# Decode attention over a sliding window: slabs of four (entry, head) pairs, a ring of three, a q projection that streams wq, and scores ordered by quadrant

## The chip, the cores and the metric

The kernel runs on one core of one Trainium2 chip. The metric is the device time of one execution in microseconds. A core has TensorE (PE in the profile; its weight loads are listed as PEld), VectorE (DVE), ScalarE (ACT), GpSimd (POOL) and SyncE (SP), which here issues nearly all DMAs. Each engine works through its own list of instructions in order and waits on semaphores. DMAs run on 16 DMA engines beside them. Data is worked on in SBUF (128 partitions); TensorE writes to PSUM, in banks of 512 fp32 per partition.

## What is computed

Two independent problems A and B of the same shape, whose results stand side by side in the output. Each is one decode step of attention with 32 query heads and 16 key/value heads for a batch of two, over the last 4096 positions of the cache.

```python
B, Sq, D = 2, 1, 576
Hq, Hkv, Sk, Dh = 32, 16, 16384, 128
W = min(4096, max(256, Sk // 4))              # 4096
q = (x @ wq).reshape(B, Sq, Hq, Dh)           # wq: 576 x 4096
k = jnp.repeat(k_cache[:, :, Sk - W:, :], 2, axis=1)
v = jnp.repeat(v_cache[:, :, Sk - W:, :], 2, axis=1)
scores = jnp.einsum("bhqd,bhkd->bhqk", q, k) * (Dh ** -0.5)
p = softmax(scores)
o = jnp.einsum("bhqk,bhkd->bhqd", p, v)
out = o.reshape(B, Sq, Hq * Dh) @ wo          # wo: 4096 x 576
```

All of it is bf16. Each key and value is used for two query heads only, so nearly all of the work is to bring in the windows of k and v: 2 problems x 2 tensors x 32 (entry, head) pairs of 1 MB.

## The kernel before

**Slabs.** A slab holds the windows of one kv head for both entries: two (entry, head) pairs, 2 MB, partition `2*r + b` holding 64 consecutive positions of entry b in one row of 16 KB. There are 32 K slabs and 32 V slabs. They go through one ring of five slots (`NR`). The order of transfers is K0, K1, ... with V(s-5) behind K(s) (`LS` = 5). SP issues them in that order (`issue_slab`, L273), and the transfer into a slot waits for the last reader of the slab that lay there: for K the last of its transposes, for V its second PV operation. The weights are threaded into the same queue: wq of A ahead of K0, wq of B in five parts (L282, L283) ahead of K7 to K11, and 1.2 MB of wo for each group of four slabs (L297). The last V slab comes in four pieces (L266).

**Scores.** K lies with positions on partitions, but the product with q needs the head dimension there. VectorE transposes blocks of 32x32 fp32 words, that is of pairs of bf16 (L844), 512 words per partition at a time, four per half slab (a unit, t). After that a partition holds a pair of dimensions of one block, and an element's position, parity and entry lie along the row. So a score matmul (L867) reads its moving operand with a step, and four of them (`p4`: two halves of the dimension, two parities) are needed for one entry of a unit. Their weights `zq` are q spread into 128 columns, nearly all zeros, so that each unit's scores land in their own rows of a PSUM bank `ST` that collects a group: eight units, four slabs.

```python
b0 = xt[:, c, o:o + 1]
mv = bass.AP(b0.tensor, b0.offset, [list(b0.ap[0]), [128, NJ], [4, 16]])
```

**Softmax** of a group: the row maximum (L378), a PE transpose (L382), a maximum over units and its negative (L392, L402), a PE broadcast (L407), its copy (L420), exp on ACT with the row sums (L428), a VectorE transpose (L476) and two products with a mask that lay the probabilities out as `pC` (L491), later the sums (L432 to L464). These steps are not done in one go: tables `pe_pre`, `da_pre`, `da_mid` and `da_post` place each of them at a unit and a quarter (t, q) of the loop (L694 to L736), so that scores and transposes of the next units stand between them on PE and VectorE.

**PV** (probability times V, L786): the weights are 16 columns of `pC`, the moving operand is 512 columns of V, and four matmuls write to four column blocks of `ACC`, side by side. It runs `LAG` = 11 units behind the transposes. ACT or VectorE copies the sum (L802, L804), four small matmuls (L758) combine the blocks into `OT`, VectorE normalises (L561).

**Projections.** q: for each group, 8 heads x 5 pieces of the dimension, wq as 128x128 weights and x as a moving operand of 56 columns, 40 matmuls (L513), then four selecting matmuls (L527) and ACT copies (L517, L545). The groups of A come at t = 0, 2, 4, 6, those of B at t = 24 to 27 and so on. Output: for each group but the last, the normalised rows are spread and redistributed (L625, L634, L646) and multiplied with wo in 16 matmuls (L658).

Of the kernel before, what the change touches and what calls it, by code (L numbers as in the profile page):

```python
# [59 lines left out]
def build_kernel(nc, probs, out, cfg=None):  # L60
    cfg = dict(cfg or {})
    NR = cfg.get("NR", 5)
    NKT = cfg.get("NKT", 3)
    NTB = cfg.get("NTB", 2)
    NZQ = 2
    ZW = 144
    LAG = cfg.get("LAG", 11)
    NPT = 3
    NS = cfg.get("NS", 56)
    LS = cfg.get("LS", 5)  # L70
    WQ_AT = cfg.get("WQ_AT", 7)
    QP_AT = cfg.get("QP_AT", 24)
    WO_LEAD = cfg.get("WO_LEAD", 5)
# [9 lines left out]
    NJ = W // 128  # L83
    assert NJ == 32
    NQ = 4
    NJ2 = 2 * NJ
    NRW = 64
    SLABW = NJ2 * 128
    UW = NJ * 128
    PP = Bb * Hkv  # L90
    NP = PP * NPROB
    ND = NP // 2
    NG = NP // 8
    GPP = PP // 8
    KP = PP // 2
    NK = NP // 2
    NFC = D // 128
    DREM = D - 128 * NFC
    assert DREM * 2 == 128
    HH = HD // 2  # L100
    NCH = NFC + 1
    NXC = NFC + 2
    NOUT = wo0.shape[1]
    NH = (NOUT + 1) // 2
    ACC0 = 128
    assert NOUT % 2 == 0 and ACC0 + NH <= 512 and NS <= 64 and NS % 2 == 0
    SCALE = float(Dh) ** -0.5
    PW = 512
    PIECES = [(0, 32), (32, 48), (48, 56), (56, 64)]

    def slab_info(D_):
        return D_ // Hkv, D_ % Hkv
# [5 lines left out]
    with es:  # L118
# [3 lines left out]
        xt = sb("xt", [128, NKT, UW], BF16)  # L122
# [3 lines left out]
        xT = sb("xT", [128, NPROB, NXC, 64], BF16)  # L126
        x_dup = sb("x_dup", [Bb, NPROB, 2, DREM, 2], BF16)
        x_sb = sb("x_sb", [Bb, NPROB, D], BF16)
        ident_b = sb("ident_b", [128, 192], BF16)
        zq = sb("zq", [128, 4, NZQ, 8, ZW], BF16)  # L130
        pR = sb("pR", [128, 2, PW], BF16)
        pT = sb("pT", [128, 2, 2 * PW], BF16)
# [3 lines left out]
        sel = sb("sel", [128, 4, 128], BF16)  # L136
        qT_sb = sb("qT_sb", [128, NG, 64], BF16)
# [8 lines left out]
        oTn = sb("oTn", [128, 2, 2, Bb], BF16)  # L146
# [3 lines left out]
        maskS = sb("maskS", [128, 8], BF16)  # L150
        selL = sb("selL", [128, 240], BF16)
        acc_sb = sb("acc_sb", [128, 2, 512], BF16)
        ident_r = sb("ident_r", [128, 72], BF16)
        pC = sb("pC", [128, NPT, 4, 2, NJ, 4], BF16)
        mask_bh = sb("mask_bh", [128, Bb, 2], BF16)
        out_sb = sb("out_sb", [Bb, NPROB, NOUT], BF16)
        ps = lambda name, shape: es.enter_context(nc.psum_tensor(name, shape, FP32))
        TB = [ps("tb%d" % i, [128, 512]) for i in range(NTB)]
        assert NTB == 2
# [9 lines left out]
        x_sems = [sem("xload%d" % P) for P in range(NPROB)]  # L169
        out_sem = sem("outdone")  # L170
        lastq_sem = [sem("lastq%d" % q_) for q_ in range(4)]
# [10 lines left out]
        p_ones_b = S.add("pool", lambda e: e.memset(ones_b[:], 1.0), [], "ones_b")  # L182
        def f_identb(e):
            e.affine_select(ident_b[:, 0:128], ones_b[:], [[-1, 128]], ALU.is_equal, 0.0, base=0, channel_multiplier=1)
            return e.memset(ident_b[:, 128:192], 0.0)
        p_ident_b = S.add("pool", f_identb, [p_ones_b], "ident_b")
        p_zqT = S.add("pool", lambda e: e.memset(qT_sb[:].rearrange("d g w -> d (g w)"), 0.0), [], "zero_qT")
        p_zxT = S.add("pool", lambda e: e.memset(xT[:].rearrange("c p h w -> c (p h w)"), 0.0), [], "zero_xT")

        def zq_zero(eng, zr_, p4s, tag):  # L190
            ops_ = []
            for p4 in p4s:
                ops_.append(S.add(eng, lambda e, p4=p4: e.memset(zq[:, p4, zr_, :, :].rearrange("d l w -> d (l w)").bitcast(FP32), 0.0),
                                  [], "%s_%d" % (tag, p4)))
            return ops_
        p_zq = {0: zq_zero("pool", 0, (2, 3), "zero_zq0p")}

        def f_sel(e):
            last = None
            for p4 in range(4):  # L200
                b32, par = p4 // 2, p4 % 2
                last = e.affine_select(sel[:, p4, :].rearrange("d (a p) -> d a p", a=4), ones_b[:, :].rearrange("d (a p) -> d a p", a=4),
                                       [[0, 4], [-2, 32]], ALU.is_equal, 0.0, base=-(64 * b32 + par), channel_multiplier=1)
            return last
        p_sel = S.add("pool", f_sel, [p_ones_b], "sel")
        p_ones_f = S.add("pool", lambda e: e.memset(ones_f[:], 1.0), [], "ones_f")
        p_ident_f = S.add("pool", lambda e: e.affine_select(ident_f[:], ones_f[:], [[-1, 128]], ALU.is_equal, 0.0,
                                                           base=0, channel_multiplier=1), [p_ones_f], "ident_f")
        for zr_ in range(1, NZQ):
            p_zq[zr_] = zq_zero("pool", zr_, (0, 1, 2, 3), "zero_zq%d" % zr_)  # L210

        p_zq[0] = p_zq[0] + zq_zero("dve", 0, (0, 1), "zero_zq0d")
        init_zero = {}
        init_zero["ST0"] = S.add("dve", lambda e: e.memset(ST[0][:], 0.0), [], "zero_ST0")
        late_zero = [("ST1", ST[1]), ("OT0", OT[0]), ("OT1", OT[1]), ("ACC0", ACC[0]), ("ACC1", ACC[1])]

        x_sem = x_sems[0]

# [7 lines left out]
        stream = []  # L226
        for s_ in range(ND + LS):
            if s_ < ND:
                stream.append(("K", s_))
            if s_ >= LS:  # L230
                stream.append(("V", s_ - LS))
        slab_idx = {key: n for n, key in enumerate(stream)}
        w_at = {}
        for P in range(NPROB):
            t0 = 0 if P == 0 else WQ_AT + 4 * GPP * (P - 1)
            for ch in range(NCH):
                w_at.setdefault(t0 + (0 if P == 0 else ch), []).append(("wq", P, ch))
        for G in range(NG):
            w_at.setdefault(4 * G + LS + (2 if by_group(G) else -1), []).append(("wo", G, 0))

        slab_dma = {}
        slab_quarters = {}
        slab_last_reader = {}
        wq_dma = {}
        wo_dma = {}
        qproj = {}
        qproj_ev = {}
        proj = {}
        next_stream = [0]

        def issue_slab(s):
            kind, D_ = stream[s]
            P, g = slab_info(D_)
            src_t = probs[P][1] if kind == "K" else probs[P][2]
            src = src_t[:, g, Sk - W:Sk, :].rearrange("b (r j) d -> r b (j d)", r=NRW)
            r = s % NR
            deps = []
            if s >= NR:
                assert slab_last_reader.get(s - NR) is not None, ("ring too small / order", s)
                deps = [slab_last_reader[s - NR]]  # L260

            if s == len(stream) - 1:
                qops = []
                for n_, (ja, jb) in enumerate(PIECES):
                    def fq(e, r=r, src=src, n_=n_, ja=ja, jb=jb):
# [64 lines left out]
        def tb_job(fn, tag, deps):  # L330
# [4 lines left out]
            if n >= NTB:  # L335
                d.append(tb_consumer[n - NTB])
# [657 lines left out]
```

## Time and profile before

| | |
|---|---|
| median of 3 runs | 373.14 us (372.84 to 373.9) |
| the profiled execution | 373.62 us |
| its span, first to last instruction | 371.8 us |
| bytes moved | 153.39 MB in 13172 packets, 413 GB/s over the span |
| PE busy | 313.2 us, 84% |
| DVE busy | 213.4 us, 57% |
| ACT busy | 30.4 us, 8% |
| mean granted TensorE clock | 0.922 |
| slab DMA of 2048 KB, issue to landing | 16.7 to 19.0 us (medians by tensor) |

A profile is one execution. Its page gives the busy time of each engine, the span in 40 equal slices (a digit is the busy share in tenths; here a slice is 9.3 us), the DMA queues, the chain of work that ended last, and the costliest groups of instructions. A group's line reads: source line, engine, operation, written from read tiles, shape, count, then busy time, mean duration in ns, and idle time ahead of it with what ended it. Matmuls overlap, so their mean duration is longer than the distance from one to the next; that distance is read from the order of time.

### The profile page before, as it was taken

Reading aid. Unit: us, or ns where it says so; the run is one execution under the profiler, and the core shown is the slowest. Engines: PE = TensorE matmul, PEld = TensorE weight load, DVE = VectorE, ACT = ScalarE, POOL = GpSimd, SP = SyncE. Lnnn points to the kernel's source line nnn. Section 1 sums busy time; section 2 is a strip of 40 time slices with the busy share of each in tenths; the row PEclk is TensorE's granted clock in tenths of the full one; section 3 lists DMA queues with packets and bytes.
Section 4 is the critical chain, followed back from the end, with each engine's and each line's share of the span. In section 5 each row is a group of like instructions: output and inputs, shape, how many; then the busy total and the mean of one; then the engine's idle time right before and its main releaser. Section 6 shows DMA issues by size and latency. Waiting matters only on the chain.

```text
span 371.8 us, 4249 instructions
## 1 busy us (share of the span) xinstructions
PE 313.2 (84%) x1764; PEld 97.3 (26%) x1764; DVE 213.4 (57%) x433; ACT 30.4 (8%) x99; POOL 6.5 (2%) x21
## 2 busy tenths in 40 slices
PE   0249997999899498999899878999699878998576
PEld 0214422222232134332223212322223222232132
DVE  3089638837853557545875557645775557726412
ACT  1100101010101001010101001010101001000111
POOL 7000000000000000000000000000000000000000
PEclk9998998999899699999989996999889996898769
DMA  7999999999999999999999999999999999999993
GB/s 310 435 430 428 427 420 361 391 386 434 420 435 428 427 425 427 420 429 428 430 429 421 428 434 425 422 432 427 425 427 430 425 427 427 425 429 413 434 414 120
DMA packets 13172, 153.39 MB, mean 413 GB/s; under 512 B 1368, under 2 KB 2400, under 8 KB 3040
## 3 DMA queue, kind: packets, MB, share of 16 engines
q1 hardware_dynamic: 13144, 153.10, 97.9%
q8 instruction: 14, 0.23, 0.3%
q14 instruction: 6, 0.05, 0.0%
q10 hardware_dynamic: 8, 0.00, 0.0%
HBM read 153.10 MB, written 0.00 MB: 412 GB/s over the span
## 4 chain that ended last, share of the span: by engine, by line
PE 46%; DMA 37%; DVE 13%; ACT 1%; issue 1%; SPq 1%
PE st L867 34%; DMA ring<-in_B_k_cache_dram 22%; DMA ring<-in_A_k_cache_dram 10%; DVE xt L844 8%; DMA ring<-in_B_v_cache_dram 5%; PE acc L786 4%; PE ot L658 3%; DVE pT L476 2%; PE tb L513 2%; DVE m L378 1%; DVE pC L491 1%; ACT pR L428 1%; PE tb L407 1%; PE tb L452 1%; PE tb L382 1%
## 5 line engine op out<-in xcount | busy, mean ns | idle before, releaser
L867 PE MATMUL st<-xt,zq 128*128 128x512 bf16 x512 | 236.0, 606 | 27.1 <-DVE xt L844 27.1
L844 DVE STREAM_TRANSPOSE xt<-ring 128x512 f32<-128x512 f32 x256 | 158.8, 675 | 53.5 <-DMA ring<-in_B_k_cache_dram 24.5
L867 PEld LDWEIGHTS st<-xt,zq 128*128 128x128 bf16 x512 | 48.9, 109 | 152.4 <-issue 108.2
L786 PE MATMUL acc<-ring,pC 128*16 128x512 bf16 x508 | 43.0, 412 | 3.5 <-DMA ring<-in_B_v_cache_dram 3.3
L561 DVE TENSOR_TENSOR oTg<-ot,rsb 128x4 bf16<-128x4 f32 x28 | 4.3, 152 | 38.0 <-PE ot L758 38.0
L802 ACT ACTIVATE acc_sb<-acc 128x512 bf16<-128x512 f32 x16 | 9.6, 597 | 143.0 <-PE acc L786 143.0
L804 DVE CAST acc_sb<-acc 128x512 bf16<-128x512 f32 x16 | 10.9, 678 | 15.1 <-PE acc L786 15.1
L476 DVE STREAM_TRANSPOSE pT<-pR 128x1024 bf16<-128x1024 bf16 x8 | 10.0, 1246 | 12.4 <-ACT pR L428 12.4
L513 PE MATMUL tb<-xT,wqb 128*128 128x56 bf16 x256 | 11.1, 198 | 6.5 <-DMA wqr<-in_A_wq_dram 6.5
L658 PE MATMUL ot<-wob,Rsb 128*2 128x288 bf16 x112 | 16.2, 302 | 0.3 <-ACT Rsb L646 0.3
L786 PEld LDWEIGHTS acc<-ring,pC 128*16 128x16 bf16 x508 | 7.9, 86 | 30.9 <-issue 23.8
L758 PEld LDWEIGHTS ot<-ident_r,acc_sb 128*128 128x128 bf16 x132 | 8.7, 106 | 20.8 <-issue 11.3
L513 PEld LDWEIGHTS tb<-xT,wqb 128*128 128x128 bf16 x256 | 10.8, 103 | 10.4 <-DMA wqr<-in_A_wq_dram 6.6
L658 PEld LDWEIGHTS ot<-wob,Rsb 128*2 128x2 bf16 x112 | 9.3, 88 | 10.1 <-issue 5.1
L378 DVE TENSOR_REDUCE m<-st 128x1 f32<-128x512 f32 x8 | 5.3, 667 | 9.7 <-PE st L867 9.7
L758 PE MATMUL ot<-ident_r,acc_sb 128*128 128x56 bf16 x132 | 9.7, 197 | 1.1 <-ACT out_sb L676 0.5
L513 PE MATMUL tb<-xT,wqr 128*128 128x56 bf16 x64 | 10.2, 197 | 0.0
L382 PE MATMUL tb<-ident_f,m 128*1 128x128 f32 x8 | 2.3, 283 | 8.6 <-DVE m L378 8.6
L545 ACT ACTIVATE zq<-tb 32x64 bf16<-32x64 f32 x32 | 7.1, 220 | 11.7 <-PE tb L527 11.5
L362 PE MATMUL tb<-ident_b,x_sb 2*128 2x2 bf16 x8 | 0.4, 161 | 7.5 <-DVE x_dup L348 7.5
L513 PEld LDWEIGHTS tb<-xT,wqr 128*128 128x128 bf16 x64 | 6.6, 103 | 0.0
L517 ACT ACTIVATE qT_sb<-tb 128x16 bf16<-128x16 f32 x8 | 1.5, 183 | 60.4 <-PE tb L513 60.4
(63 smaller groups left out, 84.6 us busy)
## 6 DMA issues: line engine op xcount, KB each, us to landing
ring<-in_A_k_cache_dram SPq DMA_DIRECT2D x16, 2048.0 KB, 18.0
ring<-in_A_v_cache_dram SPq DMA_DIRECT2D x16, 2048.0 KB, 16.7
ring<-in_B_k_cache_dram SPq DMA_DIRECT2D x16, 2048.0 KB, 17.6
ring<-in_B_v_cache_dram SPq DMA_DIRECT2D x15, 2048.0 KB, 19.0
wob<-in_A_wo_dram SPq DMA_DIRECT2D x4, 1152.0 KB, 17.1
wob<-in_B_wo_dram SPq DMA_DIRECT2D x4, 1152.0 KB, 16.9
wqb<-in_A_wq_dram SPq DMA_DIRECT2D x4, 1024.0 KB, 7.9
wqb<-in_B_wq_dram SPq DMA_DIRECT2D x4, 1024.0 KB, 15.7
```

Of the source, the lines that this page charges most:

```text
L378: chain[(G, "max")] = S.add("dve", lambda e: e.tensor_reduce(m1[:], ST[x][:, :], AX.X, ALU.max), deps, "cmax_%d" % G)
L382: n, bank, op = tb_job(lambda e, bank: e.transpose(bank[0:1, 0:128], m1[:, 0:1], ident_f[:]), "cTm_%d" % G, [chain[(G, "max")], p_ident_f])
L476: return e.transpose(pT[:, G % 2, :], src)
L513: last = e.matmul(bank[:, hl * 64:hl * 64 + NS], w_, x_, start=(ch == 0), stop=(ch == NCH - 1))
L545: last = e.activation(dst, src, ACTF.Copy)
L658: last = e.matmul(OT[half][0:Bb, ACC0:ACC0 + NH], Rsb[:, G % 2, s_, :], wob[:, G % 2, s_, half * NH:(half + 1) * NH], start=False, stop=Tr ...
L758: last = e.matmul(OT[x][:, 0:NS], acc_sb[:, x, 128 * jl4:128 * jl4 + 128], ident_r[:, 4 * jl4:4 * jl4 + NS], start=False, stop=True, skip_ ...
L786: last = e.matmul(ACC[x][32 * cb:32 * cb + 16, 0:512], pC[:, pr, gl, jh, jl:jl + 4, :].rearrange("k j c -> k (j c)"), ring[:, r, j0_ * 128 ...
L802: acc_ev[D_] = S.add("act", lambda e: e.activation(acc_sb[:, x, :], ACC[x][:, :], ACTF.Copy), d, "accev_%d" % D_)
L804: acc_ev[D_] = S.add("dve", lambda e: e.tensor_copy(acc_sb[:, x, :], ACC[x][:, :]), d, "accev_%d" % D_)
L844: xop = S.add("dve", lambda e, r=r, c=c, q=q, o=o: e.transpose(xt[:, c, q * 1024:(q + 1) * 1024].bitcast(FP32), ring[:, r, o:o + 1024].bit ...
L867: last = e.matmul(ST[x][:, 0:512], zq[:, p4, zr, 2 * gl + b, 16 - 16 * jh:144 - 16 * jh], mv, start=False, stop=True, skip_group_check=True)
```

## The change

Nearly the whole body of `build_kernel` is rewritten; the arithmetic and the bytes stay.

- **Slabs** of 4 MB: four (entry, head) pairs, pair c on partitions 32c to 32c+31, 128 positions per partition in one row of 32 KB. 16 K slabs and 16 V slabs, a ring of three, V(s-2) behind K(s). The pairs are (entry 0, head g), (0, g+8), (1, g), (1, g+8).
- **Weights**: wq in two transfers per problem, its first 512 rows with 32 KB per partition, B's ahead of K3; wo of a group ahead of K2, K4, ... (that of the last group ahead of K15). A group is now two slabs, and there are still eight.
- **q projection**: x, doubled up into 128 columns, is the weight and wq the moving operand, 512 columns a time: 10 matmuls per group into rows, two ACT copies (`qrow`), a VectorE transpose (`qtr`) and a copy (`qkeep`); then four ACT copies into `zq`. The four groups of A stand ahead of the first transpose of K, those of B in slabs 5 to 8 behind the sixth transpose.
- **Scores**: a slab is eight chunks; a chunk is one transpose of 1024 words and four matmuls. As a quadrant of partitions holds one pair, the moving operand's step is two elements. Rows of `ST` are ordered quadrant first. `ST` is no longer cleared by a memset; the first matmul of a group starts it.
- **Softmax** of a group: all of it right behind the last score of the group's second slab, in one block per engine; V of slab s-2 is multiplied inside that block on PE (`do_PV` between `do_exp` and `do_sum`). There are four products into `pC` instead of two, with a step of two in what they write.
- **PV**: 32 weight columns instead of 16; all its sums are copied by ACT; combining uses 8 columns instead of 56.
- **End**: five pieces of the last V slab; the two halves of the output lie on two partition blocks and are stored by two DMAs.

```diff
-    NR = cfg.get("NR", 5)
-    NKT = cfg.get("NKT", 3)
...
-    LAG = cfg.get("LAG", 11)
...
-    LS = cfg.get("LS", 5)
...
+    NR = cfg.get("NR", 3)
+    NKT = cfg.get("NKT", 4)
...
+    LS = 2
...
+    PIECES = [(0, 64), (64, 96), (96, 112), (112, 120), (120, 128)]
...
-            src = src_t[:, g, Sk - W:Sk, :].rearrange("b (r j) d -> r b (j d)", r=NRW)
...
+            src = src_t.rearrange("b h s d -> (b h) s d")[g::SPP, Sk - W:Sk, :].rearrange("c (r j) d -> c r (j d)", r=32)
+            r = n % NR
+            deps = [reader[n - NR]] if n >= NR else []
...
+                e.dma_start(wqb[:].rearrange("p s n -> p (s n)"),
+                            wqP[0:NFC * 128, :].rearrange("(p s) n -> p (s n)", s=NFC)).then_inc(wq_sem[P], 16)
...
+        def do_qproj(G):
...
+                    for ch in range(NFC + 1):
+                        w_ = wqb[:, ch, c0:c0 + 512] if ch < NFC else wqr[:, c0 - hf * HH:c0 - hf * HH + 512]
+                        x_ = xT[:, P, ch if ch < NFC else NFC + hf, :]
+                        last = e.matmul(bank[:, 0:512], x_, w_, start=(ch == 0), stop=(ch == NFC))
...
+                evs.append(S.add("act", lambda e, bank=bank, nb=nb: e.activation(qrow[:, 512 * nb:512 * nb + 512], bank[:, 0:512], ACTF.Copy),
+                                 d, "qrow%d_%d" % (G, nb)))
...
+            chain[(G, "qtr")] = S.add("dve", lambda e: e.transpose(qtr[:].bitcast(FP32), qrow[:].bitcast(FP32)), d, "qtr%d" % G)
...
+        def do_X(s, c):
+            issue_until(pos[("K", s)])
+            n = pos[("K", s)]
+            i = s * NC + c
+            deps = [slab_dma[n]]
+            if i >= NKT:
+                deps.append(Sop[divmod(i - NKT, NC)])
+            Xop[(s, c)] = S.add("dve", lambda e: e.transpose(
+                xt[:, i % NKT, :].bitcast(FP32), ring[:, n % NR, c * CW:(c + 1) * CW].bitcast(FP32)), deps, "X%d_%d" % (s, c))
+            if c == NC - 1:
+                reader[n] = Xop[(s, c)]
...
+        def do_S(s, c):
...
+                for p4 in range(4):
+                    o = 64 * (p4 // 2) + p4 % 2
+                    b0 = xt[:, i % NKT, o:o + 1]
+                    mv = bass.AP(b0.tensor, b0.offset, [list(b0.ap[0]), [128, JC], [2, 32]])
+                    last = e.matmul(ST[G % 2][:, 0:512], zq[:, p4, zr, sl, w0:w0 + 128], mv,
+                                    start=first and p4 == 0, stop=final and p4 == 3)
...
+        for G in range(GPP):
+            do_qproj(G)
+            if G == 0:
+                do_zq(0)
+        init_small()
+
+        for s in range(ND + 1):
+            D2 = s - 3
+            if s < ND:
+                for c in range(NC):
+                    do_X(s, c)
+                    if c >= 1:
+                        do_S(s, c - 1)
...
+                    if c == 5 and QP_AT <= s < QP_AT + (NPROB - 1) * GPP:
+                        do_qproj(GPP + s - QP_AT)
+                do_S(s, NC - 1)
+                if s % 2 == 1:
+                    do_max(s // 2)
+                    do_exp(s // 2)
+                if s >= LS:
+                    do_PV(s - LS, range(NC), None)
+                if s % 2 == 1:
+                    do_sum(s // 2)
```

The lines left out in the loop place the combining, normalising, redistribution and output matmuls of slab s-3 at chunks 1, 3, 4 and 6 of slab s.

## The prediction, made before the run

> **What bounds the kernel now.** I read the page's slices first, for the DMA rows, then the chain, then the costliest groups, and last the order in time around the places that the change touches.
>
> ```profile
> PE   0249997999899498999899878999699878998576
> DVE  3089638837853557545875557645775557726412
> ...
> DMA  7999999999999999999999999999999999999993
> GB/s 310 435 430 428 427 420 361 391 386 434 420 435 428 427 425 427 420 429 428 430 429 421 428 434 425 422 432 427 425 427 430 425 427 427 425 429 413 434 414 120
> ```
>
> The DMA engines are full from the second slice to the last but one, at some 428 GB/s. Only slices 7 to 9 sag (361 to 391). The first transfer starts at about 2.5 us and the last piece lands at 368.4, 3.4 before the end of 371.8. So DMA sets the end, and what can be gained is the sag, the edges and the cost per packet.
>
> ```profile
> PE 46%; DMA 37%; DVE 13%; ACT 1%; issue 1%; SPq 1%
> ...
> L867 PE MATMUL st<-xt,zq 128*128 128x512 bf16 x512 | 236.0, 606 | 27.1 <-DVE xt L844 27.1
> L844 DVE STREAM_TRANSPOSE xt<-ring 128x512 f32<-128x512 f32 x256 | 158.8, 675 | 53.5 <-DMA ring<-in_B_k_cache_dram 24.5
> ```
>
> The chain passes through TensorE for 46%, because a slab's slot is only reloaded once its transposes are done, and these wait for scores. PE is busy 84% of the span, 236 us of it in the scores: PE is second, and close. What one costs stands in the order of time:
>
> ```profile
> 140.57 0.27 PE L513 MATMUL tb<-xT,wqb 128*128 128x56 bf16 x4
> 140.68 0.19 PE L513 MATMUL tb<-xT,wqr 128*128 128x56 bf16 x1
> 140.70 0.27 PE L513 MATMUL tb<-xT,wqb 128*128 128x56 bf16 x4
> ...
> 205.86 3.62 PE L867 MATMUL st<-xt,zq 128*128 128x512 bf16 x8
> 209.41 0.61 PE L786 MATMUL acc<-ring,pC 128*16 128x512 bf16 x8
> ```
>
> Columns are start, duration, engine, line, form and count. Five projections of 56 columns, each with its own 128x128 weights, start every 0.13 us: 0.026 a piece, 0.46 ns per column. Eight scores take 3.62; less one's own 0.606, that is 3.01/7 = 0.43 from start to start, 0.85 ns per column, nearly twice. Weights are not the reason, the projections have the same. What differs is the moving operand: L867 reads every fourth bf16 element, 8 bytes apart. The eight PV matmuls (PV is probability times V) next to it release PE after about 0.54, 0.0675 each, as they run four side by side.
>
> **The change, part by part.** Bytes stay: 153.1 MB. So do 512 scores of 512 columns and as many PV matmuls.
>
> *DMA.* Rows go from 16 to 32 KB. In the trace's packets the medians are 159 ns for 4 KB, 309 for 8 KB, 613 for 16 KB: two halves cost 5 to 9 ns more than a whole. 248 pairs of packets per DMA engine by 7 ns: 1.7 us, nothing if the rows are cut. The sag cost (430-351)/430 of 12 us at 60 to 72 plus (430-403)/430 of 12 at 72 to 84: 2.9 us. It goes if the new ring never runs dry. If both go, DMA alone gives 371.8 - 2.9 - 1.7 = 367.2.
>
> *Transposes.* 128 of 1024 instead of 256 of 512. Four of the latter run in 2.49, 0.62 each; 512 more columns add 0.54 (the column part, 0.62 less some 0.08): 1.16, and 9.3 per slab. That lies within the 9.8 us that a slab takes to land (4.19 MB at 426.5 GB/s, the mean from 2.5 to 360).
>
> *Scores.* Stride 4 becomes 2 elements, 4 bytes. No row shows this. Bounds: 0.22 (contiguous, 0.46 ns times 512 is 0.235; the PV pairs come to 0.27 per four) and 0.433 (8 bytes apart). I take 0.433: it is the nearest row, as the operand is still not contiguous. Below 0.22 is excluded, above 0.433 too, since the operand is denser than before. [...]
>
> *Softmax between groups.* Before, it lay between scores of the next slab. Now VectorE's order is max, nM, nMrep, pT, four pC products, sums, and only then the next slab's first transpose; PE's is the transpose of m, the bias, one slab's PV, the sums, then scores. At the end of the kernel before, it stands bare:
>
> ```profile
> 346.42 0.61 PE L786 MATMUL acc<-ring,pC 128*16 128x512 bf16 x8
> 346.52 0.69 DVE L378 TENSOR_REDUCE m<-st 128x1 f32<-128x512 f32 x1 [3.96 <-PE st L867]
> ...
> 348.78 0.69 ACT L428 ACTIVATE pR<-st,bias_sb 128x512 bf16<-128x512 f32 x1
> ...
> 349.59 1.25 DVE L476 STREAM_TRANSPOSE pT<-pR 128x1024 bf16<-128x1024 bf16 x1 [1.48 <-ACT pR L428]
> 350.87 0.76 DVE L491 TENSOR_TENSOR pC<-pT,mask_bh 128x512 bf16<-128x512 bf16 x2
> ```
>
> From scores' end (346.4) to pT's start 3.15; pT is half as long, 0.62; four pC at 0.38 to 0.6, together 1.9 (now written with a stride); two sums 0.6; a transpose 1.16: **7.45 us without scores every second slab**, with only 2.2 of PV inside it.
>
> *q projection.* 320 matmuls of 56 columns become 80 of 512, contiguous: 10 per group, 2.2 to 4.3 us against 40 times 0.026 = 1.05. All four of the first problem stand before the first transpose. wq lands at 14.4 as before. PE 4.3, two ACT copies at 0.6 and the q transposes, then 2.3 per group for ACT copy, copy and transpose in turn: 27.6; ten small set-up operations of VectorE 2.6: the first transpose starts at 30.2, though K0 lands at 24.3. The second problem's stand in slabs 5 to 8: VectorE waits there for PE's ten matmuls and ACT's copies before transposes 6 and 7, so the slab is released some 7 us later.
>
> *Sum.* Per group of two slabs, PE: 64 scores 27.7, PV 2.2, combining, redistribution and the 16 output matmuls (2.05) 3.0, softmax 7.45: 40.4. DMA: four slabs 39.3 and wo 2.8: 42.1. PE can win back only 1.7 us per group. I chained the slabs by hand: a slab starts when it has landed and PE and VectorE are free; transposes run four chunks ahead of scores at most; transfer n starts 1.8 us after transfer n-3's last reader (K: last transpose, V: its PV). In us:
>
> | slab | landed | last transpose | last score | PE free |
> |---|---|---|---|---|
> | K0 | 24.3 | 39.6 | 45.3 | 45.3 |
> | K1 | 34.1 | 53.5 | 59.2 | 65.1 |
> | K2 | 46.7 | 74.9 | 80.6 | 82.8 |
> | K5 | 119.7 | 138.7 | 141.1 | 147.1 |
> | K6 | 142.1 | 164.5 | 167.6 | 169.8 |
> | K8 | 189.5 | 210.8 | 214.0 | 216.2 |
> | K15 | 342.6 | 352.3 | 358.0 | 363.9 |
>
> V5 waits for K6's release: 164.5 + 1.8, but the stream is out of work at 161.0: 5.3 us lost. V7 waits for K8: 4.3. All DMA idling is 9.7, and the stream ends at 2.5 + 359 + 9.7 = 371.2. PE is late too: after 363.9 the group before the last is finished (4.0), V14 multiplied and projected (2.2 + 2.5): 372.6, then V15's pieces 3.0, then 3.4 as before from last piece to end: **379.0**. The profiled execution took 373.62 at a span of 371.8, 1.8 more, and stands 0.5 above the median of 373.14. So 380.8, and against the median some 380.5.
>
> **Rivals.** *B, scores at the full rate*, the other side. The trace allows a fixed price per 16 bytes read: 256 such for 512 columns now, 1.69 ns each; the new stride needs 128, so 0.22 a score. Then the transposes set a slab, 9.3 us. The same chaining gives K6 released at 155.3 and K15's last score at 343.3, no DMA idling, and V13 to V15 still to land: DMA bound, 367.2, as a time 369.0. For it speaks that 1.69 ns per 16 bytes fits; against it, that 0.85 ns per element fits as well. It decides below 0.36 us a score; at 0.34 chaining gives no loss. [...] *C, between*: 0.40 a score gives 371.8 in the chaining, 373.6 as a time; also a shorter softmax path (6.5 instead of 7.45) with 0.433 ends near 374. *D, the rows are slow*: four pairs lie 32 MB apart and each DMA engine reads them at a pitch of 32 KB. Were 134.2 MB of slabs to move at the sag's 351 GB/s, 67 us would come on top: about 440. Nothing in the profile speaks for it; two pairs 64 MB apart run at 428 now. [...] *That rows are cut* costs 1.7 in B and nothing in the forecast.
>
> **How the numbers follow.** Forecast (A) 0.53, its own range 375 to 385, from a softmax path of 6.5 to 9; B 0.38, 367 to 371; C 0.06; D 0.03. A measurement of this kernel tells about 0.3% from no change, 372.0 to 374.3. Faster: B and a third of C, 0.40; same: the rest of C and A's edge, 0.05; slower: 0.55. The range must span A and B, 367 to 385; it leaves out D, and the ends of both.
>
> **What would show it.** A score's spacing in the run after: 0.43 is A, 0.22 is B. PE idle of some 5 us after every second slab. First transpose near 30. VectorE waiting between transposes 5 and 6 of slabs 5 to 8. DMA below full at 160 to 200 for A, full throughout for B. 32 KB packets, half as many. The forecast is wrong if scores go faster, or if the softmax path is much shorter than 7.45.

## The result and the profile after

The changed kernel takes 1667.7 us (median of 4 runs, 1625.5 to 1708.9) against 373.3 (372.8 to 373.9) for the kernel before: 4.37 times as long, with an interval of 4.34 to 4.39. Executions of one kernel can fall into a fast and a slow state, and this ratio and those below compare fast runs alone (here 1625.5 and 1638.9). The forecast was 380.5 in a range to 385. The profiled execution is the longest of the four, 1708.9 with a span of 1707.2; the numbers of the profile stand against that.

The page of the changed kernel, its slices (42.7 us each now) and its DMA queues:

```profile
PE   2022020200202121203021020200202102002102
DVE  1023020300102020302030020300202002003000
...
DMA  4222622222222222222222222222221122122211
GB/s 151 60 66 75 161 108 102 104 71 86 87 94 92 97 108 108 106 103 107 108 105 67 88 89 94 96 89 85 86 91 49 57 82 90 63 84 87 88 56 51
DMA packets 7332, 153.31 MB, mean 90 GB/s; under 512 B 266, under 2 KB 1302, under 8 KB 1942
...
q1 hardware_dynamic: 7306, 153.10, 25.2%
```

Before, the DMA row was 9s at 428 GB/s. Now it is 2s: on average a quarter of the 16 DMA engines works, and no slice of slabs alone gets above 108 GB/s. The compute engines are idle most of the time. The trace's packets say it more sharply: from 200 to 250 us, where only slabs move, exactly four packets are in flight for 49.4 of the 50 us. So this is not a stream that stops and waits (a few late slices apart, where the row falls to 1), and not 16 engines that are each slow: four engines work and the rest have nothing to do. The same bytes moved (153.1 MB).

The page's costliest groups:

```profile
L398 DVE STREAM_TRANSPOSE xt<-ring 128x1024 f32<-128x1024 f32 x128 | 148.0, 1212 | 1133.3 <-DMA ring<-in_B_k_cache_dram 614.4
L420 PE MATMUL st<-xt,zq 128*128 128x512 bf16 x512 | 151.3, 450 | 859.4 <-DVE xt L398 858.9
```

The last part of a line is the idle time ahead of the group and what ended it: transposes wait 1133 us in all for slabs, scores wait behind the transposes. The scores themselves got cheaper, 151 us instead of 236.

Transfers of wq, whose source has the partitions outermost, keep all 16 engines busy. Here is the stretch in which wq of A comes in, and the one of wq of B, which shares the engines with slabs (columns: stretch, length, busy time and count of PE, PEld, DVE, ACT and POOL, clock, DMA share, GB/s):

```profile
4.00:12.00 8.00, 0.50 (x12) 0.44 (x12) 0.36 (x2) 0.38 (x1) 0.00 (x0) 1.00 0.97 418
181.00:189.00 8.00, 0.00 (x0) 0.00 (x0) 0.00 (x0) 0.00 (x0) 0.00 (x0) 0.50 1.03 262
```

In the first nothing ails the engines: share 0.97, 418 GB/s, packets of 32 KB at a median of 1213 ns. In the second all are busy again, but the packets take 1948 ns in the median; why was not tried.

**The theory that follows** (theory M in the expectations below). A transfer is dealt out to DMA engines along the outermost dimension of its source. The new slab's source is `c (r j)`, four pairs outermost: four engines. The wo source is `t (p s)`, two halves outermost: two engines, and in the trace its packets of 9216 bytes are in flight one or two at a time (three for 0.7 us in all). Before, a slab's source had 64 row groups outermost: 16 engines, and from 100 to 340 us there are never fewer than 16 packets in flight. The numbers close: a 32 KB packet has a median of 1213 ns, so four engines carry 4 x 32768 / 1213 ns = 108 GB/s, the best slices. An engine now has 32 packets of each of 32 slabs, at a mean of 1474 ns: 1509 us; the two engines of wo have 64 packets of 347 ns (the median) for each of seven groups on top, 155; wq adds some 20. That is 1684 of the span of 1707.

**Rivals**, by their letters in the expectations. *R*: pairs 32 MB apart in memory make reads slow (the nearest to rival D of the prediction). *P*: what makes it slow is that several engines write to the same group of partitions, or to partitions 32 apart in SBUF, at a time. *O*: a ring of three whole slabs runs dry. For R and P speaks that 16% of the 32 KB packets take 2.0 us or more instead of 1.21. Against both, as the main cause, speaks the DMA share of 0.25, and against O that four engines work nearly without a break.

### The profile page after: what moved, and what is told of

Its sections match the earlier page's. It is cut to its first block, busy times and chain, and to the rows that moved or that the text cites. A ratio compares the mean times of both kernels' runs of the same rounds, so it can differ in the third digit from the quotient of the medians.

```text
span 1707.2 us, 3370 instructions
## 1 busy us (share of the span) xinstructions
PE 249.6 (15%) x1419; PEld 94.6 (6%) x1424; DVE 201.8 (12%) x276; ACT 37.9 (2%) x107; POOL 2.9 (0%) x10
## 4 chain that ended last, share of the span: by engine, by line
another core or an unknown queue 76%; PE 7%; SPq 7%; DVE 6%; DMA 2%; issue 1%; ACT 0%
SPq L226 7%; PE st L420 5%; DVE xt L398 4%; DMA ring<-in_B_v_cache_dram 2%; PE acc L521 1%; PE tb L354 1%; DMA wqr<-in_A_wq_dram 1%; DVE m L429 0%; DVE qtr L367 0%; ACT qrow L361 0%; PE tb L448 0%; DVE pC L477 0%; PE ot L624 0%; DVE nM L436 0%
## 5 line engine op out<-in xcount | busy, mean ns | idle before, releaser
L398 DVE STREAM_TRANSPOSE xt<-ring 128x1024 f32<-128x1024 f32 x128 | 148.0, 1212 | 1133.3 <-DMA ring<-in_B_k_cache_dram 614.4
L420 PE MATMUL st<-xt,zq 128*128 128x512 bf16 x512 | 151.3, 450 | 859.4 <-DVE xt L398 858.9
L521 PE MATMUL acc<-ring,pC 128*32 128x512 bf16 x508 | 57.1, 626 | 554.5 <-DMA ring<-in_B_v_cache_dram 321.9
L521 PEld LDWEIGHTS acc<-ring,pC 128*32 128x32 bf16 x508 | 17.2, 138 | 585.7 <-DMA ring<-in_B_v_cache_dram 326.3
L477 DVE TENSOR_TENSOR pC<-pT,maskC 128x512 bf16<-128x512 bf16 x32 | 20.5, 719 | 0.3
L354 PE MATMUL tb<-wqb,xT 128*128 128x512 bf16 x59 | 16.6, 401 | 6.6 <-DMA wqr<-in_A_wq_dram 5.2
L361 ACT ACTIVATE qrow<-tb 128x512 bf16<-128x512 f32 x16 | 9.4, 597 | 114.4 <-PE tb L354 113.4
L367 DVE STREAM_TRANSPOSE qtr<-qrow 128x512 f32<-128x512 f32 x8 | 5.7, 712 | 30.2 <-ACT qrow L361 30.2
L624 PE MATMUL ot<-wob,Rsb 128*2 128x288 bf16 x112 | 8.0, 285 | 0.3 <-ACT Rsb L602 0.3
L354 PEld LDWEIGHTS tb<-wqb,xT 128*128 128x128 bf16 x64 | 6.4, 102 | 14.8 <-DMA wqr<-in_A_wq_dram 5.3
L383 ACT ACTIVATE zq<-qk 32x16 bf16<-32x16 bf16 x32 | 6.8, 211 | 1.4 <-DVE qk L368 1.0
```

The source lines that it names most:

```text
L354: last = e.matmul(bank[:, 0:512], x_, w_, start=(ch == 0), stop=(ch == NFC))
L361: evs.append(S.add("act", lambda e, bank=bank, nb=nb: e.activation(qrow[:, 512 * nb:512 * nb + 512], bank[:, 0:512], ACTF.Copy), d, "qrow% ...
L367: chain[(G, "qtr")] = S.add("dve", lambda e: e.transpose(qtr[:].bitcast(FP32), qrow[:].bitcast(FP32)), d, "qtr%d" % G)
L383: last = e.activation(zq[pr_, :, zr, :, Z0 + 32 * a:Z0 + 32 * a + 2], qk[pr_, G, :, :].rearrange("d p (t l r) -> d p t l r", l=2, t=2)[:, ...
L398: Xop[(s, c)] = S.add("dve", lambda e: e.transpose(xt[:, i % NKT, :].bitcast(FP32), ring[:, n % NR, c * CW:(c + 1) * CW].bitcast(FP32)), d ...
L420: last = e.matmul(ST[G % 2][:, 0:512], zq[:, p4, zr, sl, w0:w0 + 128], mv, start=first and p4 == 0, stop=final and p4 == 3)
```

## The experiments

### Row groups outermost, and nothing else

```diff
-            src = src_t.rearrange("b h s d -> (b h) s d")[g::SPP, Sk - W:Sk, :].rearrange("c (r j) d -> c r (j d)", r=32)
+            src = src_t.rearrange("b h s d -> (b h) s d")[g::SPP, Sk - W:Sk, :].rearrange("c (r j) d -> r c (j d)", r=32)
...
-                    src = woP.rearrange("(t r) n -> t r n", t=2)[:, r0:r0 + 512, :].rearrange("t (p s) n -> t p (s n)", s=8)
+                    src = woP.rearrange("(t r) n -> t r n", t=2)[:, r0:r0 + 512, :].rearrange("t (p s) n -> p t (s n)", s=8)
```

> The kernel after, with only the order in which its slab and wo transfers name their rows changed: row outermost (32 rows of 4 pairs; 64 rows of 2 halves) instead of pair outermost. Rows, bytes, addresses, number of transfers and every instruction of the engines stay; the rows land on other partitions, so the scores and the output products are those of mixed-up rows. Theory M (a transfer is spread over no more DMA engines than its outermost dimension has entries: 4 for a slab, 2 for wo, as the 266 packets under 512 B, 4 per slab, 2 per wo and 16 per wq transfer, and the DMA share of 0.25 say): all 16 engines, DMA full, 365 to 371 us. Rival R (rows of 32 KB from regions 32 MB apart are slow wherever they run): over 1000 us still. Rival O (a ring of three with whole slabs leaves the DMA idle): DMA share well under 0.9, over 450 us.

Measured: 371.4 us (6 runs, 371.0 to 372.6), before 373.6: 0.9943, interval 0.9925 to 0.9962. That is 0.4 above the range expected of theory M, and far from R's and O's. Two letters exchanged in two lines take away 1296 us, all that had been lost (1294). Same pairs, same rows of 32 KB, same ring; only the order of the dimensions differs, and with it the partitions on which the rows land. The slices (9.2 us) of this kernel:

```profile
PE   0475948438093866857695864858194842905765
...
DMA  8999999999999999999999999999999999599993
GB/s 338 412 444 419 445 433 419 445 412 445 419 444 413 421 438 447 418 437 426 435 437 422 411 447 440 417 444 419 440 421 440 409 452 429 194 452 438 412 423 150
```

DMA is full again, but for slice 34, of which below. PE's row has gaps now: of the 86.5 us that VectorE idles ahead of its transposes, 86.1 end with a slab's landing (33.0 with slabs of A, 53.1 with slabs of B), so DMA sets the end.

### Two engines instead of sixteen, in the kernel before

```diff
-            src = src_t[:, g, Sk - W:Sk, :].rearrange("b (r j) d -> r b (j d)", r=NRW)
+            src = src_t[:, g, Sk - W:Sk, :].rearrange("b (r j) d -> b r (j d)", r=NRW)
```

> The kernel before, with one line changed: its slabs name the entry outermost (2 entries of 64 rows) instead of the row. Rows stay 16 KB, the ring five slots of 2 MB; rows land on other partitions, so the scores are of mixed-up rows. Theory M: two DMA engines carry each slab, at most 2 x 27 GB/s, and 134.2 MB need 2480 us or more: 2500 to 3500. Rivals R and O: nothing of the change is in it, so 373.

Measured: 2581.3 us (one run), 54 GB/s in most slices:

```profile
DMA  2111121111211111111111111111111111112111
GB/s 116 54 54 54 60 75 67 66 66 54 74 54 54 54 54 68 54 54 54 54 67 54 54 54 61 62 54 54 54 68 54 54 54 54 68 54 66 54 54 47
```

Packets of 16 KB keep their 613 ns (median 611). Two engines give 2 x 16384 / 611 ns = 53.6 GB/s, and that is the row. M holds here with another count, in another kernel, without the new pairs, rows or ring. Over the slab transfers so far, 4 outermost give 108 GB/s at best, 2 give 54, 64 and, with the row outermost, 32 give some 430.

### Pairs close together in memory

```diff
-            src = src_t.rearrange("b h s d -> (b h) s d")[g::SPP, Sk - W:Sk, :].rearrange("c (r j) d -> c r (j d)", r=32)
+            src = src_t.rearrange("b h s d -> (b h) s d")[4 * g:4 * g + 4, Sk - W:Sk, :].rearrange("c (r j) d -> c r (j d)", r=32)
```

> The kernel after, with a slab's four pairs taken from neighbouring heads, 4 MB apart, instead of 32 MB; the output is that of heads in another order. Four DMA engines still. Theory P (the packets of 2.0 to 2.6 us come of two engines that write to partitions 32 apart at the same time): a like share of slow packets, 1550 to 1750 us. Rival R (they come of the distance in memory): the share changes a good deal, below 1450 or beyond 1900.

Measured: 1711.3 us (one run), with 16.1% of slow packets against 15.9%: 4 MB or 32 MB between the pairs makes no difference. Two other runs speak against R as well. With the row outermost, the same pairs 32 MB apart are read at full rate, and the two engines of the experiment before read 64 MB apart with 1.1% of packets beyond 1.6 times the median, where the changed kernel has 16.4%. So R falls, for the distances tried. What makes the slow packets stays open: they come in stretches (62% of those that start from 50 to 100 us are beyond 1.6 times the median, none from 300 to 350 or 750 to 850), with the same four engines and the same layout throughout.

### A slab in four transfers of 32 rows

Each quadrant is filled by a transfer of its own, with its 32 rows outermost, so that 16 engines work; wo comes in two.

```diff
+            def fs(e):
+                for c in QO:
+                    last = e.dma_start(ring[32 * c:32 * c + 32, r, :], src[c]).then_inc(ring_sem[r], 16)
...
+                    for t in range(2):
+                        last = e.dma_start(wob[64 * t:64 * t + 64, pc, :, :].rearrange("p s n -> p (s n)"), src[t]).then_inc(wo_sem[pc], 16)
...
```

> The kernel after, with each slab brought in by four transfers, one per pair, each of 32 rows to 32 partitions, and wo by two of 64 rows; everything else stays. Theory M: 16 engines for each transfer, so the DMA share is near 1. Whether it is also fast tells what the packets of 2.0 to 2.6 us in the run after are (a fifth of all; most of them take 1.21): if 16 engines on the same 32 partitions get in each other's way (theory P, they share a way into SBUF), packets take about 2.4 us throughout and the time is 134.2 MB at half of 428 GB/s, 627, and with the weights 650 to 700 us; if not, 366 to 373. Rival R: over 1000 us.

Measured: 707.9 us (one run), a little above the 650 to 700 expected of theory P. The DMA share is full, and yet:

```profile
DMA  9999999999999999999999999999999999999995
GB/s 327 210 206 216 208 273 273 208 216 208 213 214 208 215 208 207 208 210 214 218 208 209 208 217 208 218 212 209 231 218 217 210 228 211 203 230 215 216 212 144
```

All 16 engines are busy and carry about half of the 430 GB/s of the run with the row outermost: packets of 32 KB have a median of 2548 ns, 93% of them are slow. So a DMA row full of 9s stands here beside 208 to 218 GB/s. The spread is mended, and a second limit appears: a packet takes 2.1 times as long with 16 engines that write the same 32 partitions at a time (2548 ns) as with 16 engines on all 128 (1213). The run with the row outermost reads the same rows of memory at full rate, and smaller transfers are not the reason either: pieces of 1 MB to all 128 partitions run at 422 GB/s in the last experiment (wq of B, 58 to 64 us). P holds for this case. Whether it also makes the slow packets of the changed kernel, where four engines write to four quadrants, this run doesn't say, nor why a packet takes longer.

### Two of the four at a time from another queue, and another order

Transfers of quadrants 0 and 1 by SyncE, those of 2 and 3 by GpSimd; and, in a second kernel, all by SyncE in the order 0, 2, 1, 3 (`QO = (0, 2, 1, 3)`).

> The kernel after, with each slab brought in by four transfers of 32 rows, the first two issued by SP and the last two by GpSimd (own semaphores); wo by two, one on each. With SP alone the packets took 2.41 us on average where 1.21 is the undisturbed value, 217 GB/s and 708 us. Theory P (the DMA engines meet on the way into the 32 partitions that all write to at one time): with two queues a DMA engine has packets for two quadrants at hand, 0 and 2, and the packets take 1.2 to 1.6 us: 370 to 480 us. Rival (DMA engines take one packet after the other and stay in step): about 700 us again.

> The kernel after, with each slab brought in by four transfers of 32 rows on SP, in the order of quadrants 0, 2, 1, 3 instead of 0, 1, 2, 3. Theory P with DMA engines in step: each transfer still fills only 32 partitions, so nothing changes, 690 to 720 us. Rival: where quadrants that share a way follow each other is what costs, and alternating them lets the engines spread: below 600.

Measured: 698.5 and 686.5 us (one run each), 220 GB/s with two queues, mean packets of 2369 and 2333 ns. The 370 to 480 us expected of two queues were wrong, and the other order comes out near the 690 to 720 expected: neither another queue nor another order relieves the limit by more than some 3%.

### What a score costs by its step

The kernel before, with the scores' moving operand stepping by 1, 2, 4 and 8 elements in turn.

```diff
-                            mv = bass.AP(b0.tensor, b0.offset, [list(b0.ap[0]), [128, NJ], [4, 16]])
+                            mv = bass.AP(b0.tensor, b0.offset, [list(b0.ap[0]), [128, NJ], [(1, 2, 4, 8)[q], 16]])
```

> The kernel before, with the step of the scores' moving operand changed: 1, 2, 4 and 8 elements in the quarters 0, 1, 2 and 3 of each unit instead of 4 everywhere, each from the unit's first columns on; the scores are those of other columns. Theory L (a fixed price per 16 bytes touched, the rival B of the prediction): distances of 0.22, 0.22, 0.43 and 0.86 us. Theory E (a price per element that is not next to the last one): 0.22 and three times 0.43. The run after has 0.216 at a step of 2, which speaks for L; a step of 8 is untried. The sum is nearly that of before with L (1.73 us for four), so some 373 us; with E 1.51, and 371 to 373.

Measured: 374.8 us (one run). The order of time has eight scores in a row, two of each step:

```profile
206.04 3.74 PE L867 MATMUL st<-xt,zq 128*128 128x512 bf16 x8
```

The single records behind that line, at a granted clock of 1.0, start 0.227 and 0.252 apart for step 1, 0.217 and 0.218 for step 2, 0.411 and 0.434 for step 4, 0.899 for step 8. Step 2 costs no more than step 1, then the price doubles with the step. That fits a fixed price for each 16 bytes that are touched (0.434 us / 256 = 1.69 ns), as rival B had it, hidden at 128 of them or fewer for 512 columns by the 0.217 that a score takes anyway. A price for each 32 bytes (0.434 us / 128 = 3.39 ns) would fit these four steps as well; a later run, with four elements in every other 16 bytes, tells the two apart. In the changed kernel eight scores with step 2 take 1.90 us at a granted clock of 1.0, again 0.217 apart:

```profile
431.99 1.90 PE L420 MATMUL st<-xt,zq 128*128 128x512 bf16 x8
```

### The sag at slice 34: a wait at the head of the queue

Row groups first had one hole left, at 312 to 324 us. SyncE's own order of time there:

```profile
319.70 0.94 SPq L255 DMA_DIRECT2D wob<-in_B_wo_dram  x2
320.68 0.55 SPq L229 DMA_DIRECT2D ring<-in_B_k_cache_dram  x1
321.28 2.65 SPq L229 DMA_DIRECT2D ring<-in_B_v_cache_dram  x2
```

The last group's wo waits for the wo buffer, that is for output matmuls on PE (23.2 us of SyncE's waiting in one piece, by the waits of its queue), and behind it waits K15, whose slot was free some 17 us earlier: in the next kernel it is issued at 302.18. V13, third in the queue, lost nothing by it, as its slot came free only with the last transpose of K14, at 319.6. The next kernel asks for this wo ahead of V14 instead of K15.

```diff
-            w_at.setdefault(2 * G + LS if by_group(G) else 2 * G + 1, []).append(("wo", G))
+            w_at.setdefault(2 * G + LS, []).append(("wo", G))
```

> The run with the row outermost, with one more edit: the last group's wo is queued ahead of V14 instead of ahead of K15. Its slot comes free only with the output product of slab 11, and in the run before this one SP stood waiting for that with K15 and V13 queued behind it; the DMA share fell to 0.64 from 312 to 324. Theory: that wait cost (430 - 246)/430 of 12 us, 5.1; the time falls by 4 to 5 us, to 366 to 368. Rival: the stream catches up or the wait moves to V14, under 1 us. As before, the rows land on other partitions, so that its scores are those of mixed-up rows.

Measured: 367.3 us (4 runs, 367.2 to 367.6), before 373.1: 0.9836, interval 0.9811 to 0.9861.

```profile
302.18 0.54 SPq L229 DMA_DIRECT2D ring<-in_B_k_cache_dram  x1
...
320.29 1.14 SPq L255 DMA_DIRECT2D wob<-in_B_wo_dram  x2
...
DMA  8999999999999999999999999999999999999992
```

This is the shortest time of the study. It is a bound and not yet a kernel: with pairs c innermost, the rows of a pair lie on every fourth partition, where the scores expect a quadrant, and wo's rows are mixed up in the same way.

### The forecast under its own conditions

The last kernel again, with the operand stepping by 4 elements, so that a score costs what the forecast took.

```diff
-                    o = 64 * (p4 // 2) + p4 % 2
+                    o = p4 % 2
...
-                    mv = bass.AP(b0.tensor, b0.offset, [list(b0.ap[0]), [128, JC], [2, 32]])
+                    mv = bass.AP(b0.tensor, b0.offset, [list(b0.ap[0]), [64, 2 * JC], [4, 16]])
```

> e8 with the scores' moving operand stepping by 4 elements instead of 2, so that a score should take the 0.43 us of the kernel before; it takes scores of other columns (entries and rows are mixed up), all else is as in e8. This gives the forecast its own conditions: full spread of the slabs, 0.43 us a score. Theory A (the chaining of the prediction is right, scores and the softmax path then make TensorE late): some 380, between 375 and 385, the DMA share below nine tenths somewhere between 100 and 230 us. Theory N (the softmax path or the projections were priced too high, DMA still sets the end): 367 to 370. Between the two the size of the miss can be read from the starts of K5 to K8.

Measured: 384.4 us, span 382.6 (one run). Its slices (9.6 us):

```profile
PE   0466994899779986999879997799959898799876
...
DMA  8999999979999999949999599999999999999993
GB/s 329 439 439 425 413 439 433 389 302 420 439 439 435 405 433 425 428 146 414 463 406 435 216 444 442 435 392 377 435 435 437 428 420 440 430 435 403 438 409 118
```

The DMA row has its holes in slice 17 (163 to 172 us) and slice 22 (210 to 220): at 430 GB/s they are worth 6.3 and 4.8 us. The prediction had lost 5.3 at 161 to 166 and 4.3 at V7. A smaller one, in slice 8 (302 GB/s, 2.8 us), it did not have. The first softmax block, from the last scores of K1 to the first of K2:

```profile
58.62 2.44 PE L420 MATMUL st<-xt,zq 128*128 128x512 bf16 x5
...
64.98 2.56 DVE L477 TENSOR_TENSOR pC<-pT,maskC 128x512 bf16<-128x512 bf16 x4
...
69.13 1.06 PE L420 MATMUL st<-xt,zq 128*128 128x512 bf16 x2 [0.50 <-DVE xt L398]
```

A score took 0.45 us here, by the records of K0 and K1 (four in 1.81), a little more than the forecast's 0.433, so the conditions are nearly but not quite its own.

### A layout for the full score rate, on two tries

The kernel before with its 64 row groups of a slab dealt out so that four neighbouring partitions hold one entry. A slab comes in four transfers, each on every fourth partition; the second kernel also queues wq of B in one go. Left out below are the pieces of the last slab, cut up in the same way, and the transpose of the probabilities and a mask, which follow the new order.

```diff
-            src = src_t[:, g, Sk - W:Sk, :].rearrange("b (r j) d -> r b (j d)", r=NRW)
+            src = src_t[:, g, Sk - W:Sk, :].rearrange("b (q l j) d -> l q b (j d)", q=16, l=4)
...
+                for l in range(4):
+                    last = e.dma_start(ring[l:128:4, r, :], src[l]).then_inc(ring_sem[r], 16)
...
-                            mv = bass.AP(b0.tensor, b0.offset, [list(b0.ap[0]), [128, NJ], [4, 16]])
+                            mv = bass.AP(b0.tensor, b0.offset, [list(b0.ap[0]), [128, NJ], [16, 4], [2, 4]])
```

> The kernel before with the rows of a slab dealt out to other partitions (8 q + 4 b + l), so that a score's moving operand finds four elements in 16 bytes instead of two; rows of 16 KB as before, four transfers of 32 rows a slab, each over 16 row groups. Theory L (fixed price per 16 bytes read): a score falls from 0.43 to 0.217 us, PE's busy time in scores from 236 to some 150 us. DMA still sets the end: the ring's sag at 72 to 96 us (2.9 us) shrinks only so far as PE caused it: 369.5 to 372.5. Theory P (transfers of 32 partitions can slow each other, as 16 engines on 32 neighbouring partitions did): packets of 16 KB above 700 ns and a time above 400.

> e11 with all of the second problem's wq queued together, at the place of its first piece. If the sag at 72 to 96 us of the kernel before comes from the order in which wq and slabs share the queue, it goes: 2.9 us less than before, 368.5 to 370.5. If it comes from late releases of the ring that faster scores have already mended, e12 equals e11 within 0.3%.

Measured: 596.1 us (4 runs, 587.0 to 602.0), 1.58 times the kernel before (1.570 to 1.595), and 576.7 (4 runs, 558.2 to 590.5). The scores do what was expected:

```profile
310.28 1.91 PE L871 MATMUL st<-xt,zq 128*128 128x512 bf16 x8
```

0.218 from start to start. Each score takes four elements out of 16 bytes and skips the next 16, so a price for each 32 bytes would give 0.43: the price is for 16. But packets of 16 KB take 1013 ns instead of 613 with all engines busy (98.9% on the queue), which is what theory P had expected. A slab in four transfers of 32 partitions is slow also when these are spread over all 128. Whether the partitions do it, or the rows of one transfer, which lie 64 KB apart in memory here and side by side before, was not tried. The second kernel can't tell anything of the sag, as its transfers are slow all along.

### The sag of the kernel before, alone

```diff
-                w_at.setdefault(t0 + (0 if P == 0 else ch), []).append(("wq", P, ch))
+                w_at.setdefault(t0, []).append(("wq", P, ch))
```

> The kernel before with all of the second problem's wq queued together, at the place of its first piece, scores as before. If the sag is one of order in the queue, it goes without faster scores: 370 to 371.5. If the ring runs dry because TensorE releases slabs late, the time stays within 0.3% of before.

Measured: 370.3 us (4 runs, 370.2 to 370.4), before 373.0: 0.9917, interval 0.9891 to 0.9943. Slices 7 to 9, at 361, 391 and 386 GB/s before, are full:

```profile
GB/s 307 433 427 425 427 426 421 430 432 425 427 427 421 427 428 426 426 431 427 428 427 421 432 428 428 417 430 430 425 427 430 425 428 430 423 428 418 427 414 135
```

The scores are as slow as before, and the slots come free as late as before. SyncE issues the same K slab at 62.63 us in the kernel before and at 62.10 in this one, after 14.5 and 12.8 us in which it issued nothing and waited for the slot. The kernel before, and then this one:

```profile
47.10 0.59 SPq L282 DMA_DIRECT2D wqb<-in_B_wq_dram  x1
...
62.63 0.54 SPq L273 DMA_DIRECT2D ring<-in_A_k_cache_dram  x1
```

```profile
46.37 2.02 SPq L282 DMA_DIRECT2D wqb<-in_B_wq_dram  x4
...
62.10 0.54 SPq L273 DMA_DIRECT2D ring<-in_A_k_cache_dram  x1
```

The difference is what the DMA engines have in hand during that wait. Here all of wq of B stands in the queue by 49 us, and its 8 KB packets fill the stream from 58 to 68 us; before, one piece was asked for at 47.10 and the others, from 68.98 on, stood behind slabs that were waiting for slots. So the ring does run short at this place, and the order of the queue decides whether there is other work to cover it. This one line is a kernel 0.8% shorter than the kernel before.

## Why the prediction was wrong

**The step that failed** is the first of the sum, *DMA*: "Rows go from 16 to 32 KB", 1.7 us for fewer packets, and with it, under *Transposes*, "the 9.8 us that a slab takes to land (4.19 MB at 426.5 GB/s, the mean from 2.5 to 360)". The packet was priced; the number of engines that carry packets was carried over from the old transfers, whose outermost dimension is 64, to the new, whose outermost is 4. A slab has 128 packets: over 16 engines 8 x 1.213 = 9.7 us, over four 38.8, and wo over two 22.5 instead of 2.8. The diff shows both sources in words, `r b (j d)` and `c r (j d)`; the forecast read them for the length of a row and for distance in memory (rival D), not for their order. In its place the runs showed four engines at 108 GB/s, two at 54 and, with the same rows in another order, 16 at some 430. No row of the trace before could have shown the price, since there the slabs ran on 16 engines (16 packets or more in flight from 100 to 340 us).

The rest of the working can be judged where the spread is mended:

- **Packets**: a 32 KB packet's median is 1213 to 1216 ns against 2 x 613: 10 to 13 ns saved for each pair, so 2.5 to 3.2 us where 1.7 was taken. DMA alone was put at a span of 367.2; it is 365.8 with row groups and wo moved. Right within 1.4 us.
- **Sag**: 2.9 us was taken; wq queued together gains 0.9917, some 3.1 us. Right in size. The ring does run dry there, as the prediction had it; a block of other work in the queue covers it.
- **Transposes**: 1.16 was taken, four take 4.62, 1.155 each. Right.
- **Scores**: 0.433 was taken, 0.217 measured. The term was twice too large; this is rival B, chance 0.38, with its price of 1.69 ns per 16 bytes. The trace before could not tell bytes from elements and shows no unit of 16 bytes, and "the nearest row" was a poor way to choose between two laws that both fitted it. The runs with steps and with blocks show the unit: with four elements in 16 bytes a score takes 0.217, with two 0.43, with one 0.90. Had only this been off, the time would have been B's 369.0; with full spread it was 371.4, and 367.3 with wo moved.
- **Softmax path**: 7.45 was taken. In the run with step 4 the last score of K1 ends at 61.06 and the first of K2 starts at 69.13: 8.07, and the other groups need 8.0 to 9.7. Four products into `pC` take 2.56 instead of 1.9; for the first group the rest fits. Too small by at least 0.6.
- **First transpose**: 30.2 was taken, it starts at 30.28 with the row outermost and at 30.65 with step 4. Right.
- **From a slot's release to the next transfer**: 1.8 was taken, an estimate of the author's that no run shows. With step 4 K6 and K8 end at 168.07 and 214.46, and the first packets after the holes start at 169.42 and 215.81: 1.35.
- **The chaining**: with 0.43 a score the forecast was a span of 379.0; 382.6 was measured. By slabs, last transposes of K1, K5, K6 and K8: 53.5, 138.7, 164.5 and 210.8 in the prediction's table, 55.1, 141.5, 168.1 and 214.5 in the trace; K15's last score 358.0 and 361.7. The chain of reasons held and runs 2 to 4 us behind. Of that, 1.6 stands already at K1, ahead of the first softmax block: 0.45 from the first transpose, the rest from a score of 0.45 instead of 0.433. What the longer softmax blocks add behind that was not parted from the scores. (The last step, 380.8 less 0.5, is 380.3 and not 380.5, which changes nothing.)
- **The wait not seen**: the last wo at the head of SyncE's queue, ahead of K15. The prediction counted this DMA's bytes, not its wait. Mending it is worth 4.0 us, 371.4 to 367.3.
- **Rival D** had the right sign and gave about 440; its mechanism, memory, was refuted by the same rows read at full rate with the row outermost, and by the pairs close together.

So theory M carries the loss. Exchanging the dimensions brings back all of the 1294 us, and in the profiled execution, which lost 1335, four engines are worth some 1050 by the working above with every packet at 1213 ns. Some 270 more come from the slow packets (1474 in the mean against 1213). Distance in memory is excluded as their cause, as far as it was varied. That the partitions make them slow is argued and not shown, as no run with four engines changed the partitions alone.

## What to carry to other kernels

Read every new or rearranged transfer for its outermost dimension before pricing its bytes: a DMA over four pairs outermost ran on four engines here (rows of 32 KB), and one over two entries or halves on two (rows of 16 and 9 KB). In these profiles it showed as a flat DMA share of 4/16 or 2/16 with most packets of normal length (medians of 1213 ns for 32 KB, 611 for 16 KB), whereas 16 engines on the same 32 partitions showed as a full share at half the GB/s (208 to 218 against some 430). And when two laws fit the one row there is (per byte, per 16 bytes, per element), the forecast should say which size of the operand tells them apart, and not lean on nearness.

## What the runs showed of the hardware that was not expected

- Rate followed the outermost dimension: 2 gave 54 GB/s, 4 at best 108, 64 and, with each transfer on all 128 partitions, 32 some 430; 16 KB packets are 611 to 613 ns with 2 engines and with 16.
- Slabs in four transfers of 32 partitions, neighbours or every fourth, slowed 16 engines down: 32 KB packets of 2548 ns instead of 1213, 16 KB packets of 1013 instead of 613. A second issuing queue did not help (220 GB/s).
- A score of 512 columns costs 0.217 to 0.25 us with a step of 1 or 2 elements, 0.41 to 0.45 with 4, 0.90 with 8; four elements out of every other 16 bytes cost 0.218.
- TensorE's granted clock fell to a mean of 0.565 in the starved kernel (0.922 before). After 63.6 us in which PE was idle it is 0.5 from 426.5 to 430.0 us and scores start 0.426 apart; from 430.0 on it is 1.0 and they start 0.217 apart.
